# Second batch's first inputs moved from the ramp into the steps, and weight blocks 8 to 15 rounded at even distances

## Chip, cores and metric

The kernel runs on one core of one Trainium2 chip. The metric is the device time of one execution in microseconds. The median of three runs of the kernel before is 2580.62 us (2579.96 to 2583.24).

## The reference

A global filter (real FFT along the sequence, product with a complex filter, inverse FFT), and behind it a two-layer block with SiLU:

```python
batch, seq, dim = (8, 3008, 256)
X = np.fft.rfft(x, axis=1)
Y = X * (filt_r + 1j * filt_i)[None, :, :]
y = np.fft.irfft(Y, n=3008, axis=1).astype(np.float32)
h = y.reshape(24064, 256) @ w_in      # 256 x 2048
g = h / (1 + np.exp(-h))
out = (g @ w_out).astype(np.float32)  # 2048 x 256
```

The inputs x and the filters are float32. The two weight matrices come as float64 (a float32 array times a NumPy double).

## The kernel before, in words

**Two kinds of work.** The spectral part turns one batch of x into y: the stages pa (or pf), pb, a product with the filter, pc and pd are chains of small matmuls with trips through DRAM between them. The block turns y into the output and is most of the time. The spectral part of batch b+1 is worked in between the block's matmuls of batch b. Only batch 0 has nothing to hide behind: its spectral part and the first weights are the ramp at the start.

**The steps.** The block's tokens are cut into pairs of column ranges (`PAIRS`, 6 per batch), the 2048 hidden channels into 8 double blocks `jp`. One pair with one `jp` is a step; a batch has 48 (`STEPS`). Both matrix products of the block use a seven-product scheme (names A11, A12, S1, S2, S3, S4, A22), so a double block of weights needs four tiles of the matrices and four combinations of them (`combine_weights`). A step has eight rounds. In step s `hidden(s)` issues the first product's seven matmuls (line 750) and `project(s-1)` the second product's seven for the step before (line 813), one of each per round, as far as a round has any. In `hidden`, by rounds:

- round 0: A11 into px; ScalarE copies px to sums[0] (line 758);
- round 1: A12 into half of pyz; VectorE adds it to sums[0], which is g0; then `finish` makes g6 and g7 of the step before (all VectorE sums have the helper's line 721);
- round 2: S2 on top of px; ScalarE copies it to sums[1] (L765) and does silu of g0 (silu0, L754);
- round 3: S1 into the other half of pyz;
- round 4: S3 on top of px; ScalarE copies it to sums[2] (L771); VectorE adds pyz to it, g2;
- round 6: A22 on top of px; ScalarE does silu3 from px and silu2 from g2;
- round 7: S4 on top of pyz's second half; VectorE adds sums[1], g1; ScalarE does silu1; VectorE makes g4 and g5 in one instruction, from g0, g1 and g2 after their silu.

px and pyz have one bank each, so A11 of the next step waits until silu3 has read px, and A12 of the next step until g1 has read pyz.

**What is put between.** `put(step, round, piece)` files a piece of other work; `until` issues it, on the engines' own queues, after that round's matmuls. With manual scheduling, each engine runs its instructions in the order in which the program issues them. Below, (1, 7) is step 1, round 7.

**Weights.** A block j of 128 hidden channels is loaded as raw 64-bit words (`load_weights`, lines 920 and 923, SP's queue). `split(j)` takes the bits apart with two VectorE instructions (lines 945 and 947) and converts both results with two ScalarE instructions, called e and m below (lines 952 and 953). `rounded(j)` makes float32 of them with three VectorE instructions (965, 967, 971), the first of which needs m. `placed(j)` multiplies the parts into the weight tile `w_t` (line 980, two VectorE instructions). Blocks 0 to 8 are rounded in the ramp and 9 to 15 in steps 0 to 6: `split` and `rounded` in round 1, `placed` in round 5 (for 9 to 11 with the four combinations of an earlier double block between `split` and `rounded`). Blocks 2jp and 2jp+1 are needed at step jp.

**Batch 1's first stage.** Its eight pieces u load 96 rows of x (`load_x`, line 277), multiply them by a table (`stage1`: two matmuls pa of 512 columns, line 335), copy the two banks to a tile t with ScalarE (line 351), and store it to DRAM (`store_rows`, four DMAs issued by POOL, line 362). A piece done in the steps also issues the load for piece u+2 (SP) and its own stores. Pieces 0 and 1 are done in the ramp, with loads issued by POOL and stores behind a copy `gate` that waits for block 8; pieces 2 to 7 in steps 1 to 6, round 3. The stage's result is read again by `load_t2` (line 443), filed at step 10, for pb at step 12.

**The ramp's end.** After the last pc of batch 0, TensorE has pieces 0 and 1 and 14 filler matmuls (`idle_wide`, line 1049), then `stage3` (pd, line 580), whose rows come back from DRAM (`load_t4_rows`, line 565). The pd banks are copied to y by ScalarE and VectorE (line 594), and step 0 needs all of y's first half. In the ramp the eight PSUM banks go round in turn (`bank`).

Of the kernel before, what the change touches and what calls it, by code (L numbers as in the profile page):

```python
# [46 lines left out]
FP32 = mybir.dt.float32  # L47
# [11 lines left out]
NJ = DFF // 128  # L59
# [8 lines left out]
A11, A12, S3, A22, S1, S2, S4 = range(7)  # L68
ROUNDS = 8
# [101 lines left out]
def kernel(  # L171
# [9 lines left out]
    nc = tc.nc  # L181
# [15 lines left out]
    def pool(name, bufs, space=None):  # L197
        kw = {} if space is None else {"space": space}
        return ctx.enter_context(tc.tile_pool(name=name, bufs=bufs, **kw))

    cpool = pool("consts", 1)
# [26 lines left out]
    w_t = cpool.tile([128, NJP, 7, 2, 128], FP32)  # L228
    warm = cpool.tile([128, 1], FP32)
    bias_t = cpool.tile([128, 5], FP32)  # L230
    gate = cpool.tile([128, 1], FP32)
    x_all = xpool.tile([128, 2, 2, 2 * C], FP32)
    x_t = [x_all[:, i] for i in range(2)]

# [376 lines left out]
    def put(step, rnd, piece, *args):  # L611

        pending.append((step + rnd / ROUNDS, len(pending), lambda: piece(*args)))
# [3 lines left out]
    def plan(b, part):  # L617

        at = STEPS * b

        if b == 1:
            for u in range(2, 8):
                put(at + u - 49, 3, part["stage1"], u)
        else:
            put(at - 72, 0, part["reverse_x"])
            for f, step, load, places in ((0, -56, -66, ((-60, 3), (-60, 5), (-59, 5), (-58, 5))),
                                          (1, -48, -55, ((-52, 3), (-52, 5), (-51, 5), (-50, 5))),
                                          (2, -40, -44, ((-42, 5), (-41, 3), (-41, 5), (-40, 3)))):
                put(at + load, 0, part["load_fold"], f)
                for k, (fold_step, rnd) in enumerate(places):  # L630
                    put(at + fold_step, rnd, part["fold"], f, k)

                put(at + step, 7, part["stage1_fold"], f)
                put(at + step, 7, part["evict_fold"], f, 0)
                put(at + step, 7, part["evict_fold"], f, 1)
                put(at + step + 1, 5, part["evict_fold"], f, 2)
                put(at + step + 1, 5, part["evict_fold"], f, 3)
            for u, step in ((6, -46), (7, -45)):
                put(at - 47, 0, part["load_x"], u)
                put(at + step, 5, part["sums"], u)  # L640
            open_step(at - 44, (part["stage1"], 6), (part["stage1"], 7))
            put(at - 44, 3, part["evict_t1"], 7, 0)
            put(at - 44, 5, part["evict_t1"], 7, 1)
        put(at - 38, 0, part["load_t2"], 0)
        put(at - 38, 0, part["load_t2"], 1)
        for g, places in enumerate((
                ((-36, 3), (-36, 5), (-35, 3), (-35, 5), (-34, 5)),
                ((-35, 6), (-34, 3), (-33, 3), (-33, 5), (-32, 1)),
                ((-32, 7), (-31, 0), (-31, 2), (-28, 5), (-27, 2)),
                ((-27, 3), (-27, 5), (-26, 3), (-25, 3), (-24, 3)),  # L650
                ((-24, 7), (-23, 0), (-23, 2), (-20, 2), (-20, 5)),
                ((-20, 3), (-19, 3), (-19, 5), (-18, 3), (-18, 5)))):
            pieces = (("forward", g), ("multiply", g, 0), ("multiply", g, 1), ("add", g, 0), ("add", g, 1))
            for (step, rnd), (piece, *args) in zip(places, pieces):
                if piece != "forward" or g in (1, 3, 5):
                    put(at + step, rnd, part[piece], *args)
        rest = 5 if b == 1 else 6
        open_step(at - 36, *last_part[0](rest), (part["forward"], 0))
        for g, step in ((0, -32), (2, -24), (4, -16)):
            put(at + step, 7, part["inverse"], g, 2)  # L660
            if g < 4:
                pending.append((at + step + 7 / ROUNDS, 10 ** 6 + 9, lambda g=g: part["forward"](g + 2, ACCS)))
                joined.add(at + step)
            put(at + step, 7, part["even"], g, 0, 2)
            put(at + step, 7, part["even"], g, 1, 2)
            put(at + step + 1, 5, part["rows"], g, 0, 2)
            put(at + step + 2, 3, part["rows"], g, 1, 2)
        put(at - 14, 5, part["load_t4"], 0)
        put(at - 14, 5, part["load_t4"], 1)
        open_step(at - 10, *alone(part, 0), (part["stage3"], 1))  # L670
        put(at - 10, 3, part["evict_y"], 1, 0)
        put(at - 10, 5, part["evict_y"], 1, 1)
        join(at - 8, part, 2, 3)
        plan_rest(b, part)

    def open_step(step, *pieces):

        opened.add(step)
        for piece, *args in pieces:
            pending.append((step - 0.06, len(pending), lambda piece=piece, args=args: piece(*args)))  # L680

    def alone(part, g, home=HIDDEN):
        return (part["stage3"], g, home), (part["evict_y"], g, 1), (part["evict_y"], g, 0)
# [5 lines left out]
    def join(step, part, *gs):  # L689

        pieces = [(part["stage3"], gs[0], ACCS), (part["evict_y"], gs[0], 0)] if gs[0] is not None else []
        for g in gs[1:]:
            pieces = [*alone(part, g), *pieces]
        for k, (piece, *args) in enumerate(pieces):
            pending.append((step + 7 / ROUNDS, 10 ** 6 + k, lambda piece=piece, args=args: piece(*args)))
        if gs[0] is not None:
            put(step + 1, 0, part["evict_y"], gs[0], 1)
        joined.add(step)
# [18 lines left out]
    v, gp = nc.vector, nc.gpsimd  # L717
    ty, g_t, acc, unfinished = {}, {}, {}, []

    def combine(eng, out, in0, in1, op):  # L720
        eng.tensor_tensor(out=out, in0=in0, in1=in1, op=op)  # L721
# [268 lines left out]
    def combine_weights(jp, part=None, eng=None):  # L990

        eng = eng or v

        def w(c):
            return w_t[:, jp, c]
        if part != 1:
            combine(eng, w(S1), w(S3), w(A22), ALU.add)
            combine(eng, w(S2), w(S1), w(A11), ALU.subtract)
        if part != 0:
            combine(eng, w(S3), w(A11), w(S3), ALU.subtract)  # L1000
            combine(eng, w(S4), w(A12), w(S2), ALU.subtract)

    def weights(*js, queue=None):
        for j in js:
            if wide:
                load_weights(j, queue)
# [9 lines left out]
    def split(*js):  # L1016
        bits(*js)
        converted(*js)

    def rounded(*js):  # L1020
        if wide:
            round_weights(*js)

    def placed(*js, eng=None):
        if wide:
            place_weights(*js, eng=eng)
        else:
            for j in js:
                load_exact(j)
# [15 lines left out]
    def idle_wide(n, ps=None, rhs=None):  # L1045

        ps = ps or bank(0, "idle")
        for _ in range(n):
            nc.tensor.matmul(out=ps[:, 0], lhsT=wx_t, rhs=wide_rows if rhs is None else rhs,
                             start=True, stop=True)  # L1050
# [5 lines left out]
    part, second = spectral(0), spectral(1)  # L1056
# [54 lines left out]
        part["inverse_first"](g)  # L1111
        part["rows_first"](g)

    for u in range(2):
        second["load_x"](u, nc.gpsimd)
    products(0)
    products(1)
    inverse(0)
# [20 lines left out]
    placed(2, 3)  # L1139
    weights(9)  # L1140
    converted(6, 7)
    for u in range(2):
        second["stage1"](u, False)
    rounded(4, 5)
    placed(4, 5)
    rounded(6, 7)
    placed(6, 7)
    split(8)
    rounded(8)
    placed(8)  # L1150
    gp.tensor_copy(out=gate, in_=w_t[:, 4, A11, 0, 0:1])
    for u in range(2):
        second["store_rows"](u)
    idle_wide(14)
    for g in range(4):
        part["stage3"](g)
    nc.sync.dma_start(out=wi_t, in_=wi_dram.ap())
    second["load_x"](2)
    weights(10, 11, 12)
    second["load_x"](3)  # L1160
    weights(13)
    early[0] = None
    plan_rest(0, part)
    for g in (4, 5):
# [2 lines left out]
        put(20, 0, lambda t=t, dram=dram: nc.sync.dma_start(out=t, in_=dram.ap()))  # L1167
    for b in range(1, B):
        plan(b, second if b == 1 else spectral(b))
    for j in range(9, NJ):  # L1170
        if j < 12:
            put(j - 9, 1, lambda j=j: (split(j), combine_weights(j - 8), rounded(j)))
        else:
            put(j - 9, 1, lambda j=j: (split(j), rounded(j)))
        put(j - 9, 5, placed, j)
        if j % 2:

            put(*((j - 8, 5) if j < 15 else (j - 9, 6)), combine_weights, j // 2, 0)
            put(*{13: (j - 8, 7), 15: (j - 8, 1)}.get(j, (j - 7, 5)), combine_weights, j // 2, 1)

        if j < 11:
            put(j - 9, 1, weights, j + 5)

    per = len(PAIRS) * 2

# [4 lines left out]
    for pair in range(len(pairs)):  # L1190
        step, rnd = combines[pair % per] if pair != 1 else (7, 5)
        pending.append((pair // per * STEPS + step + rnd / ROUNDS, 98, lambda pair=pair: tokens(pair)))
        for chunk in range(2 if pair < len(pairs) - 1 else 0):
            step, rnd = stores[pair % per][chunk]
# [56 lines left out]
```

## Time and profile before

| what | value |
|---|---|
| profiled execution, device time | 2580.55 us |
| its span, first to last instruction | 2578.7 us |
| mean granted TensorE clock | 0.996 |
| TensorE busy | 2555.9 us, 99% of the span |
| VectorE, ScalarE, POOL busy | 65%, 42%, 16% |
| DMA moved | 171.08 MB, mean 66 GB/s |
| step 0 starts (first px) | 78.87 us |
| steps 1, 2, 3, 4, 5 start at | 86.65, 95.48, 103.60, 111.71, 119.69 us |
| steps 6, 7, 8, 9 start at | 127.54, 136.19, 142.56, 148.62 us |

The starts are those of the px matmul that reads y and follows the pyz matmul on y, in the timeline of TensorE. A line of a timeline has the start, the duration, the engine, the line, the operation, output and inputs and, in brackets, how long the engine was idle before it and what ended that. Each float32 matmul appears as two records (x2). A line of the stretches has, after the length, the busy time of TensorE, weight load, VectorE, ScalarE and POOL with their instruction counts, then TensorE's granted clock, the DMA share and GB/s. A busy TensorE in these views is not TensorE at its peak: where the clock is halved, a matmul of 0.43 us takes 0.86.

### The profile page before, as it was taken

Reading aid. Unit: us, or ns where it says so; the run is one execution under the profiler, and the core shown is the slowest. Engines: PE = TensorE matmul, PEld = TensorE weight load, DVE = VectorE, ACT = ScalarE, POOL = GpSimd, SP = SyncE. Lnnn points to the kernel's source line nnn. Section 1 sums busy time; section 2 is a strip of 40 time slices with the busy share of each in tenths; the row PEclk is TensorE's granted clock in tenths of the full one; section 3 lists DMA queues with packets and bytes.
Section 4 is the critical chain, followed back from the end, with each engine's and each line's share of the span. In section 5 each row is a group of like instructions: output and inputs, shape, how many; then the busy total and the mean of one; then the engine's idle time right before and its main releaser. Section 6 shows DMA issues by size and latency. Waiting matters only on the chain.

```text
span 2578.7 us, 48117 instructions
## 1 busy us (share of the span) xinstructions
PE 2555.9 (99%) x18852; PEld 2196.2 (85%) x18852; DVE 1665.8 (65%) x3588; ACT 1086.0 (42%) x3010; POOL 421.3 (16%) x670
## 2 busy tenths in 40 slices
PE   8999999999999999999999999999999999999998
PEld 6788888888888888888888888988888888888987
DVE  7866666666666666666666666666666666555554
ACT  3544444444444444434444434444444444444443
POOL 2211111121112111311122111211121112101101
PEclk9899999999999999999999999999999999999999
DMA  8621232222222222222223222331232311210011
GB/s 277 171 62 50 71 79 63 60 64 75 60 63 69 70 62 58 76 73 64 64 59 88 51 66 58 80 80 46 66 79 65 74 42 28 64 19 16 9 17 16
DMA packets 200443, 171.08 MB, mean 66 GB/s; under 512 B 122100, under 2 KB 174180, under 8 KB 199428
## 3 DMA queue, kind: packets, MB, share of 16 engines
q1 hardware_dynamic: 179000, 117.32, 19.8%
q0 software_dynamic: 16992, 44.91, 5.5%
q10 hardware_dynamic: 4224, 5.77, 0.8%
q8 instruction: 148, 2.42, 0.4%
q14 instruction: 79, 0.65, 0.1%
HBM read 96.07 MB, written 81.26 MB: 69 GB/s over the span
## 4 chain that ended last, share of the span: by engine, by line
PE 97%; DVE 1%; DMA 1%; ACT 0%; issue 0%; SPq 0%; DVEq 0%; ACTq 0%
PE acc L813 44%; PE px L750 26%; PE pyz L750 19%; PE pd L580 3%; PE pb L457 2%; PE pc L500 2%; PE pf L424 1%; PE pc L522 0%; PE pa L344 0%; PE pa L335 0%; DMA d<-q 0%; DMA t<-d 0%; DMA raw<-in_moe_w_in_dram 0%; DVE g L721 0%; DVE w_t L721 0%
## 5 line engine op out<-in xcount | busy, mean ns | idle before, releaser
L813 PE MATMUL acc<-g,w_t 128*128 128x256 f32 (+1 forms) x5376 | 1509.2, 375 | 0.4 <-DVE g L721 0.4
L813 PEld LDWEIGHTS acc<-g,w_t 128*128 128x128 f32 x5376 | 1021.6, 190 | 115.8 <-DVE g L721 0.8
L721 DVE TENSOR_TENSOR g<-pyz,abc 128x256 f32<-128x256 f32 (+1 forms) x1152 | 479.9, 417 | 620.3 <-ACT abc L771 356.0
L721 DVE TENSOR_TENSOR g<-g 128x256 f32<-128x256 f32 (+3 forms) x1152 | 599.4, 520 | 196.7 <-ACT g L754 183.6
L750 PE MATMUL px<-ty,w_t 128*128 128x256 f32 (+1 forms) x2304 | 678.3, 376 | 1.4 <-ACT abc L765 1.0
L754 ACT ACTIVATE g<-g 128x256 f32<-128x256 f32 (+1 forms) x1152 | 472.9, 411 | 250.9 <-DVE g L721 250.9
L750 PEld LDWEIGHTS px<-ty,w_t 128*128 128x128 f32 x2304 | 432.3, 190 | 64.9 <-issue 6.2
L721 POOL TENSOR_TENSOR s<-s 128x256 f32<-128x256 f32 (+1 forms) x329 | 254.8, 792 | 1416.6 <-DVE s L833 1350.6
L750 PE MATMUL pyz<-y,w_t 128*128 128x256 f32 (+1 forms) x1536 | 454.3, 378 | 0.4 <-DVE g L721 0.4
L750 PEld LDWEIGHTS pyz<-y,w_t 128*128 128x128 f32 x1536 | 283.9, 190 | 48.2 <-DVE g L721 7.9
L765 ACT COPY abc<-px 128x256 f32<-128x256 f32 (+1 forms) x384 | 141.3, 368 | 372.8 <-PE px L750 372.8
L771 ACT COPY abc<-px 128x256 f32<-128x256 f32 (+1 forms) x384 | 141.5, 368 | 338.1 <-PE px L750 337.1
L754 ACT ACTIVATE g<-px 128x256 f32<-128x256 f32 (+1 forms) x384 | 145.8, 380 | 300.2 <-PE px L750 300.1
L750 PE MATMUL px<-y,w_t 128*128 128x256 f32 (+1 forms) x768 | 232.7, 385 | 0.8 <-DVE y L594 0.8
L750 PE MATMUL pyz<-ty,w_t 128*128 128x256 f32 (+1 forms) x768 | 225.4, 375 | 0.2 <-DVE g L721 0.2
L750 PEld LDWEIGHTS px<-y,w_t 128*128 128x128 f32 x768 | 140.6, 190 | 32.9 <-DVE y L600 5.8
L750 PEld LDWEIGHTS pyz<-ty,w_t 128*128 128x128 f32 x768 | 144.6, 190 | 18.7 <-DVE g L721 1.0
L758 ACT COPY abc<-px 128x256 f32<-128x256 f32 (+1 forms) x384 | 135.3, 352 | 53.7 <-PE px L750 53.6
L580 PEld LDWEIGHTS pd<-wi_t,t 48*64 48x64 f32 x3840 | 61.3, 135 | 26.2 <-ACT g L754 16.4
L436 POOL DMA_DIRECT2D d<-tf x144 | 71.4, 503 | 30.7 <-DVE tf L432 26.7
L863 DVE STREAM_TRANSPOSE o<-s 128x256 f32<-128x256 f32 x192 | 73.9, 423 | 1.5 <-issue 0.7
L833 ACT COPY s<-acc 128x512 f32<-128x512 f32 (+1 forms) x94 | 54.2, 577 | 47.6 <-PE acc L813 47.5
(137 smaller groups left out, 1262.4 us busy)
## 6 DMA issues: line engine op xcount, KB each, us to landing
t<-d SPq DMA_DIRECT2D x120, 192.0 KB
t<-d SPq DMA_DIRECT2D x84, 256.0 KB
d<-q POOLq DMA_DIRECT2D x84, 256.0 KB, 2.6
out_dram<-o SPq DMA_DIRECT2D x636, 32.0 KB
d<-tf POOLq DMA_DIRECT2D x144, 96.0 KB, 3.3
xr<-in_x_dram SPq DMA_DIRECT2D x6, 1472.0 KB
x_all<-in_x_dram SPq DMA_DIRECT2D x72, 96.0 KB
x_all<-xr SPq DMA_DIRECT2D x72, 96.0 KB
```

What stands on the lines that cost most here:

```text
L436: nc.gpsimd.dma_start(out=d1[k // 2, :, k % 2, n0:n0 + 4], in_=us["tf"][32 * k:32 * k + NS].rearrange("p q n c -> p (q n) c"))
L457: nc.tensor.matmul(out=ps[k][32 * j:32 * j + 32, ri, :], lhsT=d_t[rows, 4 * g + at, ri, :], rhs=rhs, start=True, stop=True)
L580: nc.tensor.matmul(out=ps[h][c0:c0 + 64, cb, i, :], lhsT=t4[rows, i, 128 * cb + c0:128 * cb + c0 + 64], rhs=wi_t[rows, :], start=True, sto ...
L721: eng.tensor_tensor(out=out, in0=in0, in1=in1, op=op)
L750: nc.tensor.matmul(out=out, lhsT=w_t[:, jp, c, 0], rhs=rhs, start=start, stop=True, skip_group_check=True)
L754: nc.scalar.activation(out=g[:, k, 0:n], in_=g[:, k, 0:n] if src is None else src, func=AFT.Silu)
L758: nc.scalar.copy(out=sums[:, 0, 0:n], in_=xo)
L765: nc.scalar.copy(out=sums[:, 1, 0:n], in_=xo)
L771: nc.scalar.copy(out=sums[:, 2, 0:n], in_=xo)
L813: nc.tensor.matmul(out=acc[pair][i][:, h, 0:n], lhsT=w_t[:, jp, c, 1], rhs=g[:, k, 0:n], start=(jp == 0 and h == 0), stop=last, skip_group ...
L833: copy(out=s[:, 2 * i:2 * i + 2, 0:n], in_=acc[pair][i][:, :, 0:n])
L863: v.transpose(out=o[:, :, h, :], in_=results[pair][:, ((2, 6), (4, 1))[chunk][h], :])
```

## The change

- Pieces 0 and 1 of batch 1 leave the ramp. Their x loads go from POOL's queue to SP's, behind the raw loads of blocks 8 and 9. All eight pieces are filed in steps 1 to 8, round 3.
- Block 8 leaves the ramp as well, and so does `gate`. Blocks 8 to 15 are filed at turns of seven rounds: `split` at (0, 1), (1, 0), (1, 7), (2, 6), (3, 5), (4, 4), (5, 2), (6, 0), `rounded` in the same round for 8 to 10 and one round later from 11 on, `placed` four rounds after the turn; the two halves of the combinations of an odd block's double block follow at four and six rounds.
- The raw loads of blocks 13 to 15 go from the ramp's end, (0, 1) and (1, 1) to (0, 5), (1, 4) and (2, 3).
- The filler grows from 14 to 24 matmuls.

```diff
-    gate = cpool.tile([128, 1], FP32)
...
         if b == 1:
-            for u in range(2, 8):
-                put(at + u - 49, 3, part["stage1"], u)
+            for u in range(8):
+                put(at + u - 47, 3, part["stage1"], u)
...
-    for u in range(2):
-        second["load_x"](u, nc.gpsimd)
     products(0)
...
     converted(6, 7)
-    for u in range(2):
-        second["stage1"](u, False)
+    second["load_x"](0)
+    second["load_x"](1)
     rounded(4, 5)
     placed(4, 5)
     rounded(6, 7)
     placed(6, 7)
-    split(8)
-    rounded(8)
-    placed(8)
-    gp.tensor_copy(out=gate, in_=w_t[:, 4, A11, 0, 0:1])
-    for u in range(2):
-        second["store_rows"](u)
-    idle_wide(14)
+    idle_wide(24)
     for g in range(4):
         part["stage3"](g)
     nc.sync.dma_start(out=wi_t, in_=wi_dram.ap())
-    second["load_x"](2)
     weights(10, 11, 12)
-    second["load_x"](3)
-    weights(13)
...
-    for j in range(9, NJ):
-        if j < 12:
-            put(j - 9, 1, lambda j=j: (split(j), combine_weights(j - 8), rounded(j)))
-        else:
-            put(j - 9, 1, lambda j=j: (split(j), rounded(j)))
-        put(j - 9, 5, placed, j)
+    turns = {8: (0, 1), 9: (1, 0), 10: (1, 7), 11: (2, 6), 12: (3, 5), 13: (4, 4), 14: (5, 2), 15: (6, 0)}
+    for j, (step, rnd) in turns.items():
+        turn = step * ROUNDS + rnd
+        put(0, turn, split, j)
+        if j < 11:
+            put(0, turn, combine_weights, j - 7)
+        put(0, turn + (j > 10), rounded, j)
+        put(0, turn + 4, placed, j)
         if j % 2:
-
-            put(*((j - 8, 5) if j < 15 else (j - 9, 6)), combine_weights, j // 2, 0)
-            put(*{13: (j - 8, 7), 15: (j - 8, 1)}.get(j, (j - 7, 5)), combine_weights, j // 2, 1)
-
-        if j < 11:
-            put(j - 9, 1, weights, j + 5)
+            put(0, turn + 4, combine_weights, j // 2, 0)
+            put(0, turn + 6, combine_weights, j // 2, 1)
+        if j in (8, 9, 10):
+            put(0, turn + 4, weights, j + 5)
```

## The prediction

> **What bounds the kernel now.** I read the page first. Its busy line, and the shares by engine of the chain that ended last:
>
> ```profile
> span 2578.7 us, 48117 instructions
> PE 2555.9 (99%) x18852; PEld 2196.2 (85%) x18852; DVE 1665.8 (65%) x3588; ACT 1086.0 (42%) x3010; POOL 421.3 (16%) x670
> PE 97%; DVE 1%; DMA 1%; ACT 0%; issue 0%; SPq 0%; DVEq 0%; ACTq 0%
> ```
>
> TensorE is the chain. From about 140 us on nothing else ends last, so matmul time and matmul waits before then reach the end one for one. The change touches only the first 160 us: the ramp to 78.87 us, where step 0 begins, and steps 0 to 8. Next, the timeline of TensorE there (start, duration, what, in brackets idle time and releaser):
>
> ```profile
> 62.49 6.21 PE L1049 MATMUL idle<-d_t,wx_t 96*128 96x256 f32 x28
> 70.25 0.28 PE L580 MATMUL pd<-wi_t,w_t 48*64 48x47 f32 x2 [1.56 <-DVE raw L971]
> 71.33 6.78 PE L580 MATMUL pd<-wi_t,w_t 48*64 48x47 f32 x254 [0.79 <-DMA raw<-in_moe_w_in_dram]
> 78.87 1.19 PE L750 MATMUL px<-y,w_t 128*128 128x256 f32 x2 [0.76 <-DVE y L594]
> ...
> 83.36 0.70 PE L750 MATMUL px<-ty,w_t 128*128 128x256 f32 x2 [0.95 <-ACT abc L765]
> 84.53 0.70 PE L750 MATMUL px<-ty,w_t 128*128 128x256 f32 x2 [0.46 <-ACT abc L771]
> 85.63 1.22 PE L750 MATMUL pyz<-y,w_t 128*128 128x256 f32 x2 [0.41 <-DVE g L721]
> ```
>
> The filler ends at 68.7; pd then waits for rows that arrive by DMA. The chain of waits gives it: the last spectrum write goes out at 59.88, lands 6.31 later, two load issues end at 67.5, the rows are there at 71.3. Step 0 waits because its sums copy (L765) stands in ScalarE's queue behind the conversion of a weight block:
>
> ```profile
> 82.44 0.61 ACT L953 ACTIVATE m<-m 128x512 f32<-128x512 uint32 x1
> 82.96 0.35 ACT L765 COPY abc<-px 128x256 f32<-128x256 f32 x1
> ```
>
> In steps 1 to 6 that wait is absent: the block's conversion comes in round 1, and the two pa matmuls of round 3 (1.72 us) cover it. One more wait matters, in step 6 (VectorE, then TensorE):
>
> ```profile
> 130.11 0.42 DVE L721 TENSOR_TENSOR g<-pyz,abc 128x256 f32<-128x256 f32 x1
> 130.58 0.70 PE L750 MATMUL pyz<-ty,w_t 128*128 128x256 f32 x2 [0.19 <-DVE g L721]
> ```
>
> The fourth hidden matmul (S1, round 3) waits until VectorE has read g0 from the other half of its bank, and starts 0.05 after it. The order with its waits says the same of every S1. Last, the clock by stretches of 1 us (TensorE's clock stands behind the busy times):
>
> ```profile
> 72.00:73.00 1.00, 1.00 (x50) 1.00 (x44) 0.18 (x1) 0.00 (x0) 0.00 (x0) 0.50 0.99 360
> 82.00:83.00 1.00, 0.41 (x2) 0.00 (x0) 0.97 (x4) 1.00 (x3) 0.00 (x0) 1.00 0.84 284
> 86.00:87.00 1.00, 1.00 (x3) 0.81 (x3) 0.35 (x2) 0.03 (x1) 0.00 (x0) 0.50 1.07 401
> ```
>
> Half clock from 71.9 to 82.0 and from 85.4 to 88.7.
>
> **What the Trainium skill says.** "TensorE: Matmul & The Clock Gate", Part 1: the clock gate looks at TensorE's activity in free-running windows of 3.41 us and halves the clock after an idle one. The trace agrees: 71.9, 82.0, 85.4 and 88.7 are 3, 1 and 1 such windows apart. It also shows that a window need not be empty: 82.1 to 85.5 had 1.7 us without a matmul, in gaps of up to 0.95, and halved the clock. The same page, "Architectural detail", calls the queues of ScalarE and VectorE strict FIFO; the L765 above is that.
>
> **The ramp, part by part.** Two pa pieces leave: 4 matmuls of 0.86, 3.45 us, at 58.95. Ten more idle matmuls of 0.43 come in: 24 x 0.432 = 10.4, so the filler ends at 69.3. pd waits for the DMA until 70.25 and 71.33 either way: worth 0. The 4 t copies (2.02 on ScalarE at 65.96) and block 8 (VectorE 72.82 to 77.1, ScalarE 73.28 to 74.5) leave too; pd has eight banks of its own and waits for neither, and step 0 waits for the last y copy, which follows the last pd: 0. POOL loses two x issues (1.29 us at 33.47), after which it waited 2.48 for VectorE, and eight store issues (3.98 at 77.4): 0. SP issues the two x loads at about 69.7, in a stretch where it was idle to 78.16, ahead of the loads of wi_t and blocks 10 to 12. 0.79 MB less moves at 33 to 45 us, where VectorE and then TensorE bind, not DMA. pd at half clock took 6.82 against 4 x 1.08 at full; the shorter gap may keep it up for a part: between 0 and -2.5, I take -0.4, since about half of the window ending at 71.9 is still empty.
>
> **The steps.** Two more pa pieces on the path: 2 x 1.72 = +3.45. Block 8 takes the place that 9 had in step 0, so step 1 begins at 86.65 as before. From there the positions decide. Prices, start to next start, from the timelines: matmul 0.432; bits 0.67, four combines 1.46, rounding 1.66, placing 0.67, g0 0.34 (0.42 to its end), finish 0.79 on VectorE; e and m 1.15, sums copy 0.25 (0.38 to its end), silu 0.32, t copy 0.47 on ScalarE; 0.63 from a matmul's start to its reader; 0.16 from an end to a full-rate matmul. I follow the queues in the order of the changed program.
>
> Step 1: block 9's bits, combines and rounding now stand at round 0, ahead of g0. VectorE takes them at 88.41, after g4 and g5 of step 0, for 0.67 + 1.46 + 1.66: g0 ends at 92.62, S1 starts at 92.78, not 90.31: 2.47. Start of step 2: 97.96.
>
> Step 2: placing and four combines delay g1 of step 1 to 99.32, A12 to 99.48: 0.66. Block 10 at (1, 7): its e and m on ScalarE wait for bits, which wait for g4 and g5, which wait for silu1 (99.78). Behind them stands the first sums copy, ending at 102.41; S2 at 102.57, not 100.34: 2.23. The rounding then holds g0 to 104.63: S1 loses 1.36.
>
> Step 3: block 11's e and m sit before silu1 and the sums copy (0.26); its rounding before g0: 114.23, S1 loses 1.58. Block 12's e and m at (3, 5) sit before silu3, which frees px for A11 of step 4: 1.70.
>
> Step 4: rounding of 12 before g1 holds A12 0.97; block 13's e and m before silu3 hold A11 0.97. Step 5: A12 0.97 again; placing and two combines before g0, S1 1.25; block 14's conversion ahead of the t copies and the third sums copy, A22 0.52. Step 6: S1 0.38. Step 7: the last combines before g1, 0.67, and 0.1 behind the t copies; step 8 0.1.
>
> These waits, with 1.07 of cold clock in step 1, sum to 3.54 + 4.25 + 3.54 + 1.94 + 2.74 + 0.38 + 0.77 + 0.10 = 17.26. Eight steps of 14 x 0.432 + 1.72 = 7.77 are 62.2; together 79.4. Before, steps 1 to 8 ran from 86.65 to 148.62, 61.97. The difference is 17.4: 3.45 of pa and 14.0 of waits.
>
> The waits now leave windows with over 2 us empty, in steps 1 to 4. Each that halves the clock costs up to half a window, 1.7; three would be 5, none 0. I take two, at some 1.3 each because a part falls under waits: +2.6.
>
> After the steps: the stores of piece 7 come in step 8, two steps later. The load of t2 stood at 137.69 for a use at 170.1, so 16 us later still fits. The outputs behind it in SP's queue went at 158.3 and nothing on TensorE waits for them soon. POOL's seven adds (5.95) stand behind four issues (1.97), most of it before their inputs arrive: 0.
>
> Sum: 17.4 + 2.6 - 0.4 = +19.6 on the profiled execution's 2580.55 (span 2578.7 and 1.85 around it; the median of the runs is 2580.62): 2600.
>
> **Rivals.** First, the cover holds: g0, the sums copies and silu3 are no later than before, and only pa is paid, 2580.55 + 3.5 = 2584. For it: steps 2 to 5 lost just 0.1 to 0.35 each. Against: the order puts rounding ahead of g0 in five steps. Second, not slower: the longer filler keeps the clock up. pd gains 2.5, the half-rate matmuls of steps 0 and 1 some 2.8, even distances the 2.2 lost in steps 2 to 7, against 3.5: 2576.5. It decides at whether the window around 70 us counts as busy; the emptier half of it speaks against. Third, half of the waits: VectorE catches up where I let delays add, 2580.55 + 3.5 + 7 = 2591. Fourth, more cold windows, each lengthening the next wait: 17.4 + 8 or so, 2606.
>
> **Numbers.** Forecast 0.66, cover holds 0.09, not slower 0.04, half 0.10, more cold 0.11. A measurement tells 0.2% (5.2 us) from no change: faster 0.03, same 0.10, slower 0.87. For 8 in 10 the range runs from just under the half case to past the cold one: 2589 to 2608.
>
> **What would show it.** Right: S1 waiting over 1 us for g0 in steps 1 to 3, S2 of step 2 waiting 2 us for the sums copy L757, A11 of step 4 waiting for silu3, and step 9 beginning 15 to 21 us later; the ramp's end unmoved. Wrong: pieces of 7.8 to 8.2 us for steps 1 to 6, or pd at full clock with step 0 near 76.4.

## The result, and the profile after

The median of four runs is 2600.31 us (2597.39 to 2601.38), against 2580.55 us for the kernel before (four runs with the profiled one, 2579.96 to 2583.24): a ratio of 1.0073, 95% interval 1.0055 to 1.009. The change makes the kernel 0.7% slower. The profiled execution is the lowest of the four, 2597.39 us; the comparison of traces below is of this one with the 2580.55 of before, so it explains 16.8 us and not the 19.8 of the medians.

The page of the kernel after, busy times and the chain by engine:

```profile
span 2595.6 us, 48151 instructions
PE 2562.6 (99%) x18872; PEld 2201.1 (85%) x18872; DVE 1665.4 (64%) x3588; ACT 1088.1 (42%) x3010; POOL 420.4 (16%) x667
PE 95%; DMA 2%; DVE 1%; ACT 1%; issue 0%; SPq 0%; ACTq 0%; DVEq 0%
```

The span grew by 16.9 and TensorE's busy time by only 6.7. The rest is TensorE waiting, and in the chain TensorE fell from 97% to 95%, with DMA and ScalarE one per cent up each. Where, the starts of the steps tell (in the views of this kernel, and of the experiments made from it, line numbers are one lower than before):

| step | 0 | 1 | 2 | 3 | 4 | 5 | 6 | 7 | 8 |
|---|---|---|---|---|---|---|---|---|---|
| starts, before | 78.87 | 86.65 | 95.48 | 103.60 | 111.71 | 119.69 | 127.54 | 136.19 | 142.56 |
| starts, after | 76.45 | 84.23 | 95.53 | 109.78 | 120.82 | 130.54 | 141.22 | 149.36 | 157.93 |
| length, before | 7.78 | 8.83 | 8.12 | 8.11 | 7.98 | 7.85 | 8.65 | 6.37 | 6.06 |
| length, forecast | 7.78 | 11.31 | 12.0 | 11.31 | 9.71 | 10.5 | 8.15 | 8.54 | 7.87 |
| length, after | 7.78 | 11.30 | 14.25 | 11.04 | 9.72 | 10.68 | 8.14 | 8.57 | 7.84 |

(The forecast is 7.77 plus the waits that the prediction gives for the step, without its 2.6 for half-clock windows in steps 1 to 4.) Steps 1 to 8 take 81.54 us instead of 61.97, +19.57. Step 0 begins 2.42 earlier. Step 9 begins at 165.77 instead of 148.62: +17.15.

TensorE's timeline from the ramp to step 1:

```profile
42.48 1.35 PE L456 MATMUL pb<-w_t,d_t 64*32 64x256 f32 x32 [1.36 <-DMA d_t<-d_tbl]
55.50 10.63 PE L1048 MATMUL idle<-d_t,wx_t 96*128 96x256 f32 x48
66.67 0.28 PE L579 MATMUL pd<-wi_t,w_t 48*64 48x47 f32 x2 [0.54 <-DMA w_t<-d]
67.76 4.98 PE L579 MATMUL pd<-wi_t,w_t 48*64 48x47 f32 x219 [0.81 <-DMA raw<-in_moe_w_in_dram]
74.94 0.78 PE L579 MATMUL pd<-wi_t,w_t 48*64 48x47 f32 x35 [2.20 <-issue]
76.45 1.19 PE L749 MATMUL px<-y,w_t 128*128 128x256 f32 x2 [0.74 <-DVE y L593]
80.95 0.70 PE L749 MATMUL px<-ty,w_t 128*128 128x256 f32 x2 [1.05 <-ACT abc L764]
90.26 0.70 PE L749 MATMUL pyz<-ty,w_t 128*128 128x256 f32 x2 [2.31 <-DVE g L720]
```

Three things are new. The filler begins at 55.50; before, the two pa pieces that stood there began at 58.95. The rows for pd arrive 3.6 earlier with it. pd is broken by 2.20 us in which TensorE waits for nothing that the profile shows ("issue"), and that gives part of the gain back: step 0 begins 2.42 earlier, not 3.6. And S1 of step 1 (the last line) now waits 2.31 for g0, the forecast's first wait. VectorE's timeline shows why:

```profile
88.12 0.68 DVE L964 SCALAR_TENSOR_TENSOR m<-raw,m 128x512 f32<-128x512 uint32 x1
88.72 0.42 DVE L966 TENSOR_SCALAR e<-e 128x512 uint32<-128x512 f32 x1
89.18 0.69 DVE L970 SCALAR_TENSOR_TENSOR e<-raw,e 128x512 uint32<-128x512 uint32 x1
89.79 0.42 DVE L720 TENSOR_TENSOR g<-pyz,abc 128x256 f32<-128x256 f32 x1
```

The three instructions that round block 9, and before them its bits and four combinations (from 85.99 on), stand ahead of g0, and S1 starts 0.05 after g0 has ended. The second of the large waits is in step 2, in ScalarE's timeline and then TensorE's:

```profile
97.08 0.42 ACT L753 ACTIVATE g<-g 128x256 f32<-128x256 f32 x1 [1.52 <-DVE g L720]
98.59 0.72 ACT L951 ACTIVATE e<-e,bias_t 128x512 f32<-128x512 uint32 x1 [1.09 <-DVE e L944]
99.22 0.61 ACT L952 ACTIVATE m<-m 128x512 f32<-128x512 uint32 x1
99.74 0.35 ACT L757 COPY abc<-px 128x256 f32<-128x256 f32 x1
```

```profile
100.15 1.22 PE L749 MATMUL px<-ty,w_t 128*128 128x256 f32 x2 [1.91 <-ACT abc L757]
104.28 3.07 PE L334 MATMUL pa<-x_all,wx_t 96*128 96x512 f32 x4
```

silu1 at 97.08 feeds g4 and g5, these feed the bits of block 10, these feed e and m, and only behind m comes the sums copy for which S2 waits, 1.91. The pa of this step then takes 3.07 where it took 1.88 at full clock (in step 1 here, and in the same step of e8 below): the clock. The stretches of one clock window each (length, busy times of TensorE, weight load, VectorE, ScalarE and POOL, then the granted clock):

```profile
96.43:99.84 3.41, 1.26 (x5) 0.68 (x4) 2.89 (x8) 1.66 (x4) 0.00 (x0) 1.00 0.66 229
99.84:103.25 3.41, 2.91 (x6) 1.93 (x7) 3.34 (x9) 1.04 (x3) 0.00 (x0) 0.50 0.00 0
103.25:106.67 3.42, 3.42 (x6) 1.78 (x6) 0.57 (x2) 0.44 (x1) 0.00 (x0) 0.50 0.01 2
```

The waits leave 2.15 of the first window without a matmul, and the clock is halved for the next two, not one. The forecast length left half clock out, and step 2 is 2.25 longer than it. The third kind of wait, silu3 behind block 12, also in step 4 as forecast, ScalarE and TensorE:

```profile
119.89 0.61 ACT L952 ACTIVATE m<-m 128x512 f32<-128x512 uint32 x1
120.40 0.36 ACT L753 ACTIVATE g<-px 128x256 f32<-128x256 f32 x1
```

```profile
120.82 0.70 PE L749 MATMUL px<-y,w_t 128*128 128x256 f32 x2 [1.36 <-ACT g L753]
122.67 0.70 PE L749 MATMUL pyz<-y,w_t 128*128 128x256 f32 x2 [0.72 <-DVE g L720]
```

The first is A11 of step 4; the second, A12 of that step, is 0.72 late because the rounding stands ahead of g1. TensorE's waits in steps 0 to 8, summed (total, times, longest):

```profile
PE pyz L749 <- DVE g L720: 7.9, 9, 2.3
PE px L749 <- ACT g L753: 2.1, 2, 1.4
PE px L749 <- ACT abc L757: 1.9, 1, 1.9
PE px L749 <- ACT abc L764: 1.1, 1, 1.1
```

Of these only the last was there before at over half a microsecond (0.95).

### The profile page after: what moved, and what is told of

It is laid out like the page before. It is cut to its first block, busy times and chain, and to the rows that moved or that the text cites. A ratio compares the mean times of both kernels' runs of the same rounds, so it can differ in the third digit from the quotient of the medians.

```text
span 2595.6 us, 48151 instructions
## 1 busy us (share of the span) xinstructions
PE 2562.6 (99%) x18872; PEld 2201.1 (85%) x18872; DVE 1665.4 (64%) x3588; ACT 1088.1 (42%) x3010; POOL 420.4 (16%) x667
## 3 DMA queue, kind: packets, MB, share of 16 engines
q8 instruction: 148, 2.42, 0.4%
## 4 chain that ended last, share of the span: by engine, by line
PE 95%; DMA 2%; DVE 1%; ACT 1%; issue 0%; SPq 0%; ACTq 0%; DVEq 0%
PE acc L812 43%; PE px L749 25%; PE pyz L749 19%; PE pd L579 3%; PE pb L456 2%; PE pc L499 2%; PE pf L423 1%; PE pa L334 1%; DMA w_t<-in_x_dram 0%; PE pa L343 0%; PE pc L521 0%; DMA raw<-in_moe_w_in_dram 0%; DVE w_t L720 0%; DMA filt<-in_filt_i_dram 0%; DVE g L720 0%
## 5 line engine op out<-in xcount | busy, mean ns | idle before, releaser
L757 ACT COPY abc<-px 128x256 f32<-128x256 f32 (+1 forms) x384 | 135.4, 353 | 53.0 <-PE px L749 53.0
```

Source lines behind the costliest of these rows:

```text
L757: nc.scalar.copy(out=sums[:, 0, 0:n], in_=xo)
```

## Experiments

Theory: the cost is in the positions. The weight work stands in VectorE's and ScalarE's queues ahead of the sums that TensorE needs next; pa adds its own 3.45 and no more. Rival: the cost is in what was taken from the ramp or from pa's new steps, and the turns are innocent. The kernels ran in three groups (e1 to e4; e5 to e8; e9 and e10), each beside the kernel before on the same chip; its medians there were 2579.97, 2580.0 and 2579.87.

Each trace is one execution, and where its half-clock windows fall differs from one to the next. Kernels with the same instructions up to a point show how much that makes: the kernel before, e2 and e10 have the same ramp, and their step 0 began at 78.87, 77.94 and 75.56 us. So a difference of 2 or 3 us at the end of the ramp in one pair of traces proves little, and the medians and the pattern over all traces count.

| kernel | median us | ratio to before, 95% |
|---|---|---|
| e1_pa_only | 2581.14 | 1.0006 [0.9998, 1.0015] |
| e2_turns_only | 2595.36 | 1.0062 [1.005, 1.0075] |
| e3_round_late | 2591.87 | 1.005 [1.0037, 1.0063] |
| e4_x_early | 2599.34 | 1.0077 [1.0064, 1.0089] |
| e5_x_mid | 2576.91 | 0.9988 [0.9982, 0.9995] |
| e6_x_mid_fill | 2576.68 | 0.9988 [0.9981, 0.9995] |
| e7_x_late | 2579.44 | 0.9996 [0.9988, 1.0004] |
| e8_block10 | 2595.05 | 1.0055 [1.0042, 1.0069] |
| e9_x_mid_comb | 2576.84 | 0.999 [0.9983, 0.9996] |
| e10_turns_whole | 2593.2 | 1.0056 [1.0042, 1.007] |

**e1_pa_only: the changed kernel with the weight blocks where they were.**

```diff
+    split(8)
+    rounded(8)
+    placed(8)
...
-    turns = {8: (0, 1), 9: (1, 0), 10: (1, 7), 11: (2, 6), 12: (3, 5), 13: (4, 4), 14: (5, 2), 15: (6, 0)}
+    for j in range(9, NJ):
...
```

> The move of the pa pieces, the x loads and the filler as in the changed kernel, with the weight blocks where the kernel before has them (8 in the ramp, 9 to 15 in rounds 1 and 5). If the positions of the blocks make the loss: two more pa pieces, +3.5 us, and the ramp 2.4 us earlier as in the changed kernel, so 2581 to 2583 us, with steps 2 to 8 at 7.8 to 8.7 us each. Rival, the pa move itself makes most of it (later stores, t copies in two more steps): 2590 or more.

Measured: +1.2 on before, as expected, with an interval that includes no change. Steps 1 to 8 take 7.80, 8.24, 8.11, 7.97, 7.85, 8.65, 7.98 and 7.84. Only steps 7 and 8 have grown by more than 0.12, by 1.61 and 1.78: two pa pieces. Step 0 begins at 75.62. So nearly all of the change's cost is in the turns and in block 8's move; pa costs what was forecast, and the ramp gives part of it back.

**e2_turns_only: the kernel before with blocks 9 to 15 at the changed turns.** This kernel leaves out the four combinations of double block 1, which the output needs, and no weight block at all is worked in its step 0 (before, block 9 was; in the kernel after, block 8 is). Its step 0 is therefore lighter than that of either kernel.

```diff
-    for j in range(9, NJ):
...
+    turns = {9: (1, 0), 10: (1, 7), 11: (2, 6), 12: (3, 5), 13: (4, 4), 14: (5, 2), 15: (6, 0)}
...
```

> The kernel before, with blocks 9 to 15 at the turns of the changed kernel; pieces 0 and 1, block 8 and the filler stay in the ramp. If the positions make the loss: steps 1 to 8 take about 16 us more than before (19.6 less 3.45 of pa), 2594 to 2598 us, with the waits of S1 for g0 in steps 1 to 3. Rival, the turns are harmless without the pa move: 2580 to 2583.

Measured: +15.4, within the expectation. Steps 1 to 8 take 79.02, 17.05 more than before; step 2 takes 13.76 of it, and steps 1, 3, 4 and 5 take 11.09, 11.04, 11.40 and 10.68. Step 0 takes 5.73. The turns alone, without block 8's move and without the two pa pieces, make most of the loss. The rival falls with e1 and e2. The parts add up to about the whole: 1.2 of e1, 15.4 of this kernel and the 2.05 by which its step 0 is shorter are 18.6 of 19.8.

**e10_turns_whole: e2 with those combinations put back.**

```diff
+        if j == 9:
+            put(0, 1, combine_weights, 1)
...
```

> As e2_turns_only, whose step 0 left out the combinations of double block 1, with these put back at (0, 1). Steps 1 to 8 take 16 to 17 us more than before as in e2_turns_only; step 0 takes 7.8 as before, not 5.7, so 2595.4 rises by 1 to 2: 2597. Rival, part of the waits in steps 1 to 3 came from the earlier start of step 1: 2594 or less.

Measured: +13.3. In its trace steps 1 to 8 take 79.33, +17.4, somewhat more than expected (14.04, 11.05, 9.72 and 10.68 in steps 2 to 5). But step 0 took 4.73 where before it took 7.78, and the expectation of 7.8 was wrong for two reasons. It overlooked that block 9's conversion and rounding are no longer in step 0 either, so that the wait for L765 (0.95 before) is gone. And TensorE was at full clock all through step 0; the clock was halved at 86.7 to 90.2 instead, in step 1 (12.78). The kernel after and e4 tell the two apart, because their steps 0 have the same instructions: 7.78 with half clock in it, 6.63 without. By that measure some 1.15 of the 3.05 is the clock, and the rest the missing block. The total fell where the rival had it, almost 4 under the theory's, and the steps where the theory had them. The Trainium skill ("TensorE: Matmul & The Clock Gate", Part 1) calls the window free-running and the transition variable from run to run; the traces agree, with 7.78 and 6.63 for one and the same step 0. How the windows fall in the unprofiled runs isn't seen, and so a total within some 3 us can't be split by one trace each.

**e3_round_late: the changed kernel with the rounding of blocks 9 to 12 behind g0.**

```diff
-        put(0, turn + (j > 10), rounded, j)
-        put(0, turn + 4, placed, j)
+        late = {9: (1, 1), 10: (2, 1), 11: (3, 1), 12: (4, 1)}
...
```

(The pieces of the four blocks go to these places; placing and the first combinations are no earlier than them.)

> The changed kernel with the rounding of blocks 9 to 12 filed in round 1 of steps 1 to 4, so behind g0 and the finish of the step; the splits stay. If S1 and A12 wait because of the rounding ahead of g0 and g1: the S1 waits of steps 1 to 3 shrink by 1.6, 1.2 and 1.35, A12 of step 4 by 0.7, and without them at least one half-clock window goes, about 2: 2600 falls to 2592 to 2595. The wait of S2 in step 2 for the sums copy (1.9) and of A11 in step 4 for silu3 (1.4) stay. Rival, only the splits matter: 2598 or more.

Measured: 8.4 less than the changed kernel, at 2591.87, just under the expectation. Steps 1 to 4 fell from 11.30, 14.25, 11.04 and 9.72 to 9.64, 12.44, 9.62 and 8.73. Waits of TensorE in the same steps:

```profile
PE pyz L749 <- DVE g L720: 3.7, 5, 1.1
PE px L749 <- ACT g L753: 2.2, 2, 1.5
PE px L749 <- ACT abc L757: 1.9, 1, 1.9
```

The waits for g fell from 7.9 to 3.7, and the two for ScalarE did not move, since `split` stayed where it was. That separates the two causes: rounding ahead of g0 and g1, and e and m ahead of a copy or silu.

**e8_block10: the changed kernel with block 10 at (2, 1).**

```diff
-    turns = {..., 10: (1, 7), ...}
+    turns = {..., 10: (2, 1), ...}
```

> The changed kernel with block 10 alone moved from (1, 7) to (2, 1), where its conversion stands behind the first sums copy. If that position makes the wait of S2 in step 2 and the S1 wait behind it, and these two the half clock of step 2: step 2 falls from 14.25 us to 8.4 to 9, and 2600 to about 2594.5. Rival, the combinations ahead of g1 or the bank of pyz hold step 2 anyway: 2598 or more.

Measured: step 2 fell from 14.25 to 8.56, and the wait for L757 is gone; that part of the expectation held. The total fell by 5.3, to 2595.05, near the expected. But in the trace steps 1 and 4 came to 13.01 and 11.37, 1.7 longer each: the clock was now halved at 92.4 to 95.7 and at 119.8 to 123.1. The profiled execution, 2597.32, is one of the two slowest of the five, so these two windows need not be in the others. That the missing wait moved them there isn't shown.

**e4_x_early: the changed kernel with the x loads where they were, on POOL's queue early in the ramp.**

```diff
+    for u in range(2):
+        second["load_x"](u, nc.gpsimd)
     products(0)
...
-    second["load_x"](0)
-    second["load_x"](1)
```

> The changed kernel with its two x loads issued by POOL at the old place, about 33 us. If the earlier end of the ramp comes from the 0.79 MB taken out of that stretch, the table d_t for pb of groups 4 and 5 lands some 2 us later again, the clock halves after that wait, step 1 begins at 86 to 87 instead of 84.2 us, and the time rises by 2 to 3: about 2602. Rival, the earlier end is chance of that execution: no change within 1.5 us.

Measured: 2599.34, no difference from the changed kernel: the rival's number, and the expected total was missed. Its trace shows why. First the pb of group 4 in the kernel before, then TensorE's timeline of e4:

```profile
44.63 2.08 PE L457 MATMUL pb<-w_t,d_t 64*32 64x256 f32 x32 [3.01 <-DVE w_t L479]
```

```profile
43.66 2.08 PE L456 MATMUL pb<-w_t,d_t 64*32 64x256 f32 x32 [2.23 <-DMA d_t<-d_tbl]
70.29 5.80 PE L579 MATMUL pd<-wi_t,w_t 48*64 48x47 f32 x254 [0.96 <-DMA raw<-in_moe_w_in_dram]
76.82 0.67 PE L749 MATMUL px<-y,w_t 128*128 128x256 f32 x2 [0.73 <-DVE y L593]
```

With the x loads early, this pb starts at 43.66, not 42.48, and runs at half clock, 2.08 instead of 1.35; the filler begins at 58.1, 2.6 later. The loads do hold up d_t. But pd is whole: the gap of 2.20 is gone, and step 0 begins only 0.37 later than in the changed kernel. Two effects of moving the loads cancel. The trace shows a third thing: step 1 ran at full clock here and took 11.27, with a wait of 3.24 for g0; in the changed kernel it was partly at half clock, waited 2.31 and took 11.30. So half clock in that step only filled a wait for VectorE that was there anyway.

**e7_x_late: e1 with the x loads behind pd.**

```diff
-    second["load_x"](0)
-    second["load_x"](1)
...
     nc.sync.dma_start(out=wi_t, in_=wi_dram.ap())
+    second["load_x"](0)
+    second["load_x"](1)
```

> As e1_pa_only with the x loads of pieces 0 and 1 behind the load of wi_t, so issued after pd, not before it. If these loads make the gap of 2.2 to 3.6 us in pd in which TensorE waits for nothing that the profile shows (its instructions, fetched by DMA): the gap goes and the time falls by 2 to 3, 2578 to 2579. Rival, the gap comes from elsewhere: it stays, 2581.

TensorE's timeline of e1, then of e7:

```profile
66.59 3.43 PE L579 MATMUL pd<-wi_t,w_t 48*64 48x47 f32 x219 [0.83 <-DMA raw<-in_moe_w_in_dram]
73.58 1.30 PE L579 MATMUL pd<-wi_t,w_t 48*64 48x47 f32 x35 [3.56 <-issue]
```

```profile
67.51 6.11 PE L579 MATMUL pd<-wi_t,w_t 48*64 48x47 f32 x254 [1.09 <-DMA raw<-in_moe_w_in_dram]
74.37 1.19 PE L749 MATMUL px<-y,w_t 128*128 128x256 f32 x2 [0.76 <-DVE y L593]
```

The gap of 3.56 is gone when the loads are behind pd, and step 0 begins 1.25 earlier. The median, 2579.44, is 0.4 over the expected range and 1.7 under e1's; but the two ran on different chips, and the intervals of their ratios overlap, so the trace shows the gap's cause better than the times do. (In the two profiled executions e7 had lost the gain again by step 9, with half clock up to 85.8 where e1's ended at 79.7.) The gap is there in all four kernels that issue these loads on SP just ahead of pd (2.20, 3.56, 2.5 in e3, 2.5 in e8), and of the others the longest is 1.01 (e6). What TensorE waited for in it stands in the last section.

**e5_x_mid: the kernel before with its x loads later, but ahead of the last blocks' loads.**

```diff
+    second["load_x"](0)
+    second["load_x"](1)
...
-    for u in range(2):
-        second["load_x"](u, nc.gpsimd)
```

(The added lines stand behind the loads of weight blocks 6 and 7, on SP's queue; they go out at 43.86.)

> The kernel before with one edit: the two x loads go from POOL at about 33 us to SP, behind the raw loads of blocks 6 and 7 (about 46 us). If the loads at 33 us hold up the table d_t and so pb of groups 4 and 5: pb of group 4 begins at 41 to 42.5 instead of 43.7 to 44.6 us, the half clock behind it goes, the ramp's filler ends 2.5 to 3.5 us earlier, and as no x load is in flight when pd begins there is no gap in pd: 2577 us against 2580. Rival, the DMAs of that stretch delay something else by as much (the spectrum writes, the row loads): no change.

```profile
40.47 1.14 PE L457 MATMUL pb<-w_t,d_t 64*32 64x256 f32 x32
66.07 0.28 PE L580 MATMUL pd<-wi_t,w_t 48*64 48x47 f32 x2 [1.88 <-DMA w_t<-d]
68.07 7.07 PE L580 MATMUL pd<-wi_t,w_t 48*64 48x47 f32 x254 [1.72 <-DMA w_t<-d]
75.91 1.19 PE L750 MATMUL px<-y,w_t 128*128 128x256 f32 x2 [0.77 <-DVE y L594]
```

Measured: 2576.91, as expected, 0.9988 of before with an interval under 1: this one part of the change, with the loads in another place, beats both kernels. pb starts 4.16 earlier than in the kernel before, without a wait, pd has no gap, and step 0 begins 2.96 earlier. Nothing but these two loads moved. Over all twelve traces the pattern is the same: with the loads at about 33 us this pb starts at 43.66 to 44.63, after a wait of 2.23 to 3.33 that three of the four traces put down to d_t; with the loads at 43 us or later it starts at 40.47 to 42.48. The issuing itself can be left out as a cause: in the kernel before, POOL's two issues end at 34.8, and POOL then waits 2.48 for VectorE. So the wait before pb came from the transfers that the loads had held up.

**e6_x_mid_fill: e5 with 20 filler matmuls instead of 14**, so that TensorE would be busy up to pd.

```diff
-    idle_wide(14)
+    idle_wide(20)
```

> As e5_x_mid with 20 filler matmuls instead of 14, so that TensorE is busy until the rows for pd arrive. If the gap ahead of pd makes the half clock there: pd at full clock for at least its first half, up to 2.5 us below e5_x_mid, about 2575.5. Rival, pd's small matmuls do not keep the clock up in any case: equal to e5_x_mid within 1 us.

```profile
PE px L750 <- DVE y L594: 2.2, 1, 2.2
PE pd L580 <- issue: 1.0, 1, 1.0
```

Measured: 2576.68, the same as e5: the rival's number, but not its reason. In the trace most of pd did run at full clock (218 of its matmuls in 3.43), and yet step 0 began at 75.34, only 0.57 earlier than in e5: it waited 2.2 for the last copy of y. On VectorE that copy stands behind the placing of block 8, which ended at 74.28. The faster pd only turns into a wait for VectorE.

**e9_x_mid_comb: e5 with the combinations of double block 1 in the ramp, ahead of block 8.**

```diff
+    combine_weights(1)
     split(8)
...
-            put(j - 9, 1, lambda j=j: (split(j), combine_weights(j - 8), rounded(j)))
+            put(j - 9, 1, lambda j=j: (split(j), j > 9 and combine_weights(j - 8), rounded(j)))
```

> As e5_x_mid with the four combinations of double block 1 moved from step 0 into the ramp, ahead of block 8, where VectorE waits 1.98 us for block 8's data. If these 1.46 us of VectorE ahead of g2 hold S4 in step 0, step 0 falls from 8.05 to about 6 us, and e5_x_mid's 2577 to 2575. Rival, ScalarE's conversion ahead of the sums copy holds step 0 anyway, or block 8 and the y copies come later by as much: 2577.

```profile
74.40 0.67 PE L750 MATMUL px<-y,w_t 128*128 128x256 f32 x2 [1.18 <-DVE y L594]
78.26 0.70 PE L750 MATMUL px<-ty,w_t 128*128 128x256 f32 x2 [1.21 <-ACT abc L765]
```

Measured: 2576.84, the rival's number. In the profiled run step 0 began at 74.40 and took 6.26, near the 6 that was expected, but because it was at full clock: e4's step 0, with its combinations and at full clock, took 6.63. The wait for L765 is still there at 1.21, since it comes from e and m and not from the combinations, and the y copy is 1.18 late. No gain over e5.

## Why the prediction was right, and where not

**The positions: right.** Every large wait that the prediction placed is in the trace at its place, with one exception: S1 of step 2, forecast to wait 1.36, waited 0.19, since TensorE was at half clock and its own matmuls took up that time. The small one of step 3 (0.26, sums copy) isn't there. After taking off the 2.42 by which step 0 came earlier, S1 of step 1 was forecast at 90.36 and came at 90.26, S2 of step 2 at 100.15 and came at 100.15. The lengths of seven of the eight steps are within 0.3 of the forecast. e3 and e8 take the two kinds of wait away one at a time. e2 and e10 show that the turns alone cost steps 1 to 8 17.1 and 17.4, although the two pa pieces are not in them. Both sums hold half-clock windows too, so they aren't the waits alone. That step 0 took 7.78 as forecast is luck: e4's, with the same instructions, took 6.63.

**pa: right.** 3.45 was forecast; steps 7 and 8 of e1 are 1.61 and 1.78 longer, 3.39.

**The half clock in the steps: mechanism right, distribution wrong.** The prediction took two windows in two places at 1.3 each, 2.6. The trace has two in a row in step 2, worth 14.25 - 12.0 = 2.25. The window of 99.84 to 103.25 was 2.91 busy and did not bring the clock back.

**The ramp: this step failed.** "0.79 MB less moves at 33 to 45 us, where VectorE and then TensorE bind, not DMA" was wrong. I took the releaser that the line names, VectorE's w_t, for the only one. The wait ended with a DMA, the table d_t, as the kernel after, e2, e4 and e10 name it and as e5 shows by moving loads only; a wait for several semaphores shows one of them. pb came 2.15 earlier and took 1.35 instead of 2.08, and the matmuls behind pc began 3.45 earlier. The other half of that step, that the x loads on SP's queue at 69.7 cost nothing, failed too: they went out at 66.08, and pd has a gap of 2.20. The prediction's -0.4 for pd and "the ramp's end unmoved" became -2.42 in the traces. That size is uncertain, since the same ramp ended at 75.56 to 78.87 in the traces of before, e2 and e10; the direction is not, since e5's median is 3.1 under before, and e1's only 1.2 over it in spite of 3.4 of pa.

**Sum.** 17.4 + 2.6 - 0.4 = 19.6 was forecast; the profiled execution shows 19.57 for the steps and -2.42 for the ramp, 17.15 at step 9 and 16.8 at the end. The median is 19.8 above before, so its nearness to the forecast is partly luck: the three unprofiled runs took 2.2 to 4.0 more than the profiled one. The record has each run's mean granted clock: 0.996 for the profiled run and 0.995 for the other three, and 0.001 of 2600 us is 2.6 us. So more half clock in these three is likely; no trace shows where it fell.

**The rivals.** "The cover holds" (2584) falls: e1 is what it describes, and only with the old turns. "Not slower" (2576.5) rested on the clock around 70 us; it was halved from 69.1 to 72.5 all the same. Its sign, step 0 near 76.4, did come, at 76.45, but from the earlier pb and not from pd at full clock. "Half of the waits" (2591) would need VectorE to catch up; it does not, as the lengths of steps 3 to 5 show. "More cold windows" (2606) falls as well: steps 2 to 8 have two, and the slowest run took 2601.38.

## What to carry to other kernels

Even distances between pieces of side work are no aim in themselves: what counts is which instruction of the main chain stands next behind each piece on the same engine, and a piece goes right behind such an instruction, not ahead of it. Of a wait that ends at two things, the named one may be the innocent; move the other's transfer and look. And a filler or a faster stage pays only if everything that the next stage waits for also comes sooner (e6). Last, before a difference of a few us between two traces is explained, look at what the same instructions took in others: here one ramp ended 3.3 us apart in three of them.

## What was unexpected of the hardware

- **Half of a bank.** S1 writes the half of the pyz bank that g0 does not read, and yet waits for g0 (start 90.26, g0's end 90.21). The Trainium skill, "PSUM — Partial Sum Buffer", section on PSUM bank collisions, says that two engines must not be in one bank and the same partitions at the same time, even at different addresses. In this program such a pair of matmul and sum is a chain, and what delays the sum delays the matmul by the same time. The skill's rule fits the waits here. The trace shows a wait for VectorE's semaphore, so the program orders the two; no run here leaves that wait out or puts the two halves into two banks.
- **The clock.** The busy time of a window alone does not tell what the next one gets. In the kernel after, a window of 1.26 busy out of 3.41 was followed by half clock and one of 1.75 (86.20 to 89.62) by full clock, but one of 1.90 (79.38 to 82.79) by half:

```profile
79.38:82.79 3.41, 1.90 (x7) 0.71 (x5) 3.34 (x9) 2.19 (x5) 0.00 (x0) 1.00 0.86 282
82.79:86.20 3.41, 3.00 (x8) 2.46 (x8) 2.28 (x7) 1.55 (x4) 0.00 (x0) 0.50 0.55 166
86.20:89.62 3.42, 1.75 (x8) 1.19 (x7) 3.35 (x9) 1.50 (x3) 0.00 (x0) 1.00 0.00 0
89.62:93.03 3.41, 2.77 (x9) 1.71 (x10) 1.34 (x4) 1.00 (x2) 0.00 (x0) 1.00 0.00 0
```

A few matmul records can be missing from a trace, and what counts as activity stays open.
- **The gap in pd.** 2.2 to 3.6 us without a releaser, in each kernel whose SP queue had the x loads right ahead of pd, and at most 1.0 in the others. The traces show what TensorE waited for. Among the DMA packets are some of the kind "instruction", and one of 16 KB moves during pd. Its line in the kernel after, for the stretch 72.2 to 73.6 (packets, MB, share of 16 engines):

```profile
q8 instruction: 1, 0.02, 5.3%
```

| kernel | last matmul ahead of the gap starts | instruction packet | next matmul starts | after the packet's end |
|---|---|---|---|---|
| after | 72.50 | 72.34 to 73.54 | 74.94 | 1.40 |
| e1 | 69.79 | 71.07 to 72.31 | 73.58 | 1.27 |
| e3 | 72.42 | 72.66 to 73.85 | 75.28 | 1.44 |
| e8 | 72.26 | 72.40 to 73.55 | 75.00 | 1.45 |
| e6 | 71.11 | 69.92 to 70.95 | 72.36 | 1.41 |
| e2 | 75.54 | 73.66 to 74.76 | 76.04 | 1.28 |

In all six TensorE goes on 1.27 to 1.45 after the packet has landed, however long it has stood. It also stops at a fixed place of its instructions: behind 220 or 221 records of pd where 24 filler and pa matmuls stand ahead (24 fillers, or e6's 20 and four of pa), and behind 232 in e2, where there are six matmuls, so twelve records, fewer. In e7 the packet landed at 71.00, and the matmul at that place started at 72.35 without a gap. So TensorE waits there, as far as traces can show it, for its next instructions. e6 has the gap although its packet isn't late, because pd at full clock reaches that place sooner. The packet starts 5.6 to 6.5 after the first pd matmul in the four kernels with the x loads right ahead of pd, and 2.7 to 5.0 after it in the other eight, so the loads hold it up. In what way, when it goes by another queue (q8), isn't shown.
